# Stage tiles in two rings, and a smaller share for attention at a hand-over

## The chip, the cores and the metric

The kernel runs on one core of one Trainium2 chip, in one launch. The time is device microseconds from a run's start to its end, the median of several runs. The time of before is 606.85 us, the median of 3 runs (605.4 to 607.78).

## The reference

One input `x` (2048 tokens of 512 channels, fp32) goes through two branches that are mixed by a gate. Cut to what matters:

```python
g = sigmoid((x * gate_w).sum(-1, keepdims=True))
# branch A: 32 heads of 16; each token attends to 8 tokens, 2 apart
q, k, v = split(x @ wqkv)
idx = pos[:, None] - 2 * arange(8)[None, :]
logits = where(idx >= 0, (q * k[idx]).sum(-1) * 16 ** -0.5, -1e9)
a = ((softmax(logits)[..., None] * v[idx]).sum(window)) @ wo
# branch B: gated feed-forward (FFN), 512 -> 1792 -> 512
b = (gelu(x @ w_gate) * (x @ w_up)) @ w_down
out = g * a + (1 - g) * b
```

## The kernel before

**Halves.** The tokens are worked on in two halves, `par` 0 and 1 (the even and the odd of 16 tokens that share a partition), since a window with step 2 never leaves its half. The program runs `start()` (keys and queries of the first half), `ffn(0)`, `kq_second()` (keys and queries of the second half), `ffn(1)` and its end with the output projection.

**Matmuls.** Every fp32 operand is split into a high and a low part (`hi` on ScalarE, `lo` on VectorE), and a product is three matmuls: high by high, low by high, high by low. The gate and up products, the keys and queries, and the values are each computed with a seven-product scheme (Strassen and Winograd's), so that sums of weights and of products (`c12`, `c22` by `add`, L566; copies `p5` and `u2` by `copy`, L561) pass through ScalarE and VectorE between the matmuls.

**The FFN.** `ffn(par)` (L704) runs over 14 chunks of 128 hidden channels. `gate_up` (L620) issues the seven products of one chunk in four PSUM banks of ring `p`, with the Gelu (`c11`, L656; `ge`, L675) and `hidden` (L571: the product L572, its high part L574 on ScalarE, its low part L575 on VectorE) behind them. The seventh product is held back to the next chunk (`fourth`). From the third chunk on, four calls of `down` (L590; matmuls at L601) for chunks that are done lie between the products. After the last chunk eight more calls of `down` follow; their sums are scaled on ScalarE (L612 in the first FFN).

**Values.** In the first two chunks of each FFN the values of the same half are computed too, by `values` (L271) along `PLAN`. Each of four token tiles `t` has two stages of 512 columns. Each stage gets three of the scheme's seven steps and is stored to memory twice: `first` (L226) stores its left part, `second` (L231) its right one, to `vs`. `STAGES` (L197) says from which rings a tile's two stages are taken: tile 2 and tile 3 take both from ring `s`. The order of the steps is, chunk by chunk (letters are steps, figures are tiles; steps d, c and e use stage 0, steps b, f and g stage 1):

```python
PLAN = (("a0 b0", "c0 d0 a1", "e0 f0 d1", "b1 g0 c1", "e1 f1 a2", "d2 g1 c2 b2"),
        ("f2 e2 a3", "g2 d3", "b3", "c3 e3", "f3", "g3"))
```

**Rings.** A ring is a fixed number of tiles of one size: `s` has 4 (512 columns), `c` has 4 (544 columns). A new tile can be written when all that used an old one of its ring is done, stores to memory included. Ring `s` serves `p5` and `u2` of every chunk; ring `c` serves `c11`, `c12`, `c22` and `ge` of every chunk, and four raw weight tiles of the values.

**Attention.** It is one long generator, `attention` (L422), over eight units (half, quarter of the channels), nearly all on VectorE. A unit has `scores` (four steps: a product L324 and a reduction L327), a softmax, and `mix` (L371; four steps: a product L386, then sums L390, L392, L394; a transpose and a store after every second). Each step yields about its cost in us: 4.6 for a step of the scores, 2.3, 1.2 and 1.1 for a step of `mix`, 0.7 for a transpose. The generator also loads: `load_kq` brings a unit's keys and queries, ahead of time if they are there.

**Who gets how much.** Everywhere in the program, `pull(budget)` (L464) adds to a credit and draws the generator until the credit is used up; `pull(1e9, key)` draws until a unit is done, and sets the credit to 0. In the FFN the budget is a fixed number times `PACE`: 0.9 in the first chunks and 1.0 later in the first FFN, 1.12 in the second. The last chunk of the first FFN has a further 0.8 in `gate_up`. In `kq_second` the blocks ask as `ASK` says. The products L324 and L386 also wait for the last matmul that was traced before them (`paced`, `LAST`), so the place in the program is a hard bound for them.

**The order on each engine** is made ahead of the run by a scheduler with a simulated timeline. It takes what is ready by its place in the program, with attention's instructions 150 places later (`BEHIND`), and deals out the tiles of the rings; the engines then run their queues in that order.

**Around the hand-over.** `ffn(0)` ends with eight `down` calls. Four of them accumulate in ring `p`, which the next stage needs too: `kq_second` (L1252) computes a first block (24 matmuls into the `acc` banks), copies the sums into four banks of `p` on ScalarE (`out_of`, L937) and adds a second block there (24 matmuls, `a12` by `b21`). Keys of the first columns are then copied to tile `kq` by `put` (L1279). The same tile holds the values that units (0, 0) to (0, 2) mix from.

Of the kernel before, what the change touches and what calls it, by code (L numbers as in the profile page):

```python
# [22 lines left out]
FC = F // P  # L23
# [8 lines left out]
NU = D // UC  # L32
# [1 line left out]
FILLERS = 2  # L34
ASK = (0.3, 0.3, 0.3, 0.6, 1.0, 1.2, 1.2)
BEHIND = 150
PACE = (0.9, 1.0, 1.12)
LOAD = 4.0
BT = 4
MASKED = -1e9 * DH ** 0.5  # L40
# [8 lines left out]
def tile_gated_mix(ctx: ExitStack, tc: tile.TileContext, xt, wqkv, wff, wo, out):  # L49
# [11 lines left out]
    def tl(tag, dt=F32):  # L61
        return pool.tile([P, COLS.get(tag, 512)], dt, name=tag, bufs=BUFS[tag])
# [5 lines left out]
    def bank(tag):  # L68
        return psum.tile([P, 512], F32, name=tag, bufs=BUFS.get(tag, 1))
# [7 lines left out]
    for i in range(WARM):  # L77
        c = i // 4 % 2 * QW
# [115 lines left out]
            VR["t4"] = VR["b21"]  # L194
            sub(VR["t4"], VR["b21"], VR["t2"])

    STAGES = (("r", "r"), ("hh", "hl"), ("s", "s"), ("s", "s"))  # L197

    def value_steps(par, t):

# [14 lines left out]
        def staged(i):  # L215
            if ("s", i) not in T:
                T["s", i] = tl(STAGES[t][i])[:, :512]
            return T["s", i]
# [72 lines left out]
    def load_kq(par, u):  # L291
        hh, c = divmod(u, 2)
        k, q = slots_of(u > 0), KQ["a"][:, 2 * NP - 1:]
        if u == 1:
            q = pool.tile([P, 2, BT * UC], F32, name="tb").rearrange("p a (b c) -> p (a b) c", c=UC)
        LG[par, u] = k, q
        if not u:
            return
        loads = load_slots(k, KS[par, hh][c])
        loads.append(nc.sync.dma_start(q, QS[par, hh][c].rearrange("(p j) d -> p j d", j=NP)))  # L300
        if not par and 1 < u < NU - 1:
            for ins in loads:
                after(ins, SCORED[-1])
        elif (par, u) == (1, 2):
            after(loads[-1], PEAK[-1])
# [13 lines left out]
    def scores(par, u):  # L319
        k, q = LG[par, u]  # L320
        lg = pool.tile([P, UH, NP, W], F32, name="lg", bufs=2)
        for jj in range(0, NP, 2):
            prod = pool.tile([P, 2, W, UC], F32, name="prod")
            paced(nc.vector.tensor_tensor(prod, spans(k, jj), q[:, jj:jj + 2, None, :].to_broadcast([P, 2, W, UC]),  # L324
                                          op=OP.mult))
            yield 2.3
            nc.vector.tensor_reduce(two_of(lg, jj), prod.rearrange("p j w (h d) -> p (j w) h d", d=DH), axis=AX.X,  # L327
                                    op=OP.add)
            yield 2.3
        first = lg[:1, :, :NP - 1, :W - 1]  # L330
        SCORED[:] = [nc.vector.tensor_tensor(
            first, first, mask[:1, None, :NP - 1, :W - 1].to_broadcast([1, UH, NP - 1, W - 1]), op=OP.min)]
        LG[par, u] = lg
# [71 lines left out]
    done = set()  # L405
# [9 lines left out]
    def ordered(ins, other):  # L415
        after(ins, other, mybir.DependencyClass.NoSync)

    def need(*key):
        while key not in done:
            yield None  # L420

    def attention():  # L422
        units = [(0, u) for u in range(NU)] + [(1, u) for u in range(NU)]
        yield from need(0, 0)
        load_kq(0, 0)
        load_kq(0, 1)
        yield from scores(0, 0)
        yield from scores(0, 1)
        yield from need(0, 1)
        scored, mixed = 2, False  # L430
        for i, un in enumerate(units):
            if scored == i:
                yield from need(un[0], un[1] // 2 * 2)
                load_kq(*un)
                if un[1]:
                    yield LOAD
                else:
                    load_kq(un[0], 1)
                yield from scores(*un)
                scored += 1  # L440
                mixed = False
            yield from softmax(*un)
            if un == (1, 0):
                yield from scores(*units[scored])
                scored += 1
                yield from need(un[0], 1)
            yield from gated(*un)


            to = units[scored] if scored < len(units) else None  # L450
            ahead = to and (to[0], to[1] // 2 * 2) in done
            if ahead:
                load_kq(*to)
            yield from mix(*un, LOAD if mixed else 0.0)
            done.add((*un, "o"))
            mixed = not ahead
            if ahead:
                yield from scores(*to)
                scored += 1

    fill = attention()
    credit = [0.0]

    def pull(budget, key=None):  # L464
        credit[0] += budget
        while credit[0] > 0 and (key is None or key not in done):
            with tc.high_priority(offset=-BEHIND):
                c = next(fill, None)
            if c is None:
                credit[0] = 0.0  # L470
                return
            credit[0] -= c
        if key:
            credit[0] = 0.0
# [105 lines left out]
    def pace(par, f):  # L580
        return PACE[2 if par else f > 5]

# [4 lines left out]
    NG = FC // 2  # L587
    out_v = out.rearrange("(p j) d -> j p d", j=NT)

    def down(par, gr, t, b):  # L590
        if b == t == gr == 0:
            ACC.update((t, bank(f"acc{t}")) for t in range(BT))
        pp = bank("p") if b else ACC[t]
        if b and gr:
            nc.scalar.activation(pp, RT[BT + t], AF.Copy)
        ts = slice(t * P, (t + 1) * P)
        for i in range(2):
            hh_, hl_ = Hs[2 * gr + i, b]
            d = WD[2 * gr + i]
            for n, (a, w) in enumerate(((hh_, d[:, :512]), (hh_, d[:, 512:1024]), (hl_, d[:, :512]))):  # L600
                ins = nc.tensor.matmul(pp, a[:, ts], w, start=(i == 0 and n == 0 and gr == 0),  # L601
                                       stop=(i == 1 and n == 2), skip_group_check=True)
                if gr and b == t == 0 and not par:
                    ordered(ins, LAST[-1])
                LAST[:] = [ins]
        jj = BT * b + t
        if gr == NG - 1 and par:
            nc.scalar.activation(pp, pp, AF.Copy, scale=gc[:, par, jj:jj + 1])
            ACC[jj] = pp
        elif gr == NG - 1:  # L610
            st = tl("rt" if b else "scss"[t])[:, :512]
            nc.scalar.activation(st, pp, AF.Copy, scale=gc[:, par, jj:jj + 1])  # L612
            nc.gpsimd.dma_start(out_v[2 * jj], st)
        elif b:
            if gr == 0:
                RT[BT + t] = tl("rt")
            nc.scalar.activation(RT[BT + t], pp, AF.Copy)  # L617
        pull(1.2 * pace(par, 2 * gr + 2))

    def gate_up(par, f, pieces, do, extra):  # L620


        w = {op: WG.pop((f, op)) for ops in GROUPS for op in ops}

        def idle(i, n):
            for x in do.get(i, ()):
                x()
            pull(n * pace(par, f) * (1.0 if par or f + 1 < FC else 0.8))

        def piece(i):  # L630
            for x in pieces[i]:
                x()

        idle(0, 0.0)
        X_ = bank("p")
        product(X_, "a11", w["b11"], True)
        W_ = bank("p")
        nc.scalar.activation(W_, X_, AF.Copy)
        next(extra, None)
        idle(1, 0.7)  # L640
        piece(0)
        Z_ = bank("p")
        product(Z_, "s1", w["t1"], True)
        p5 = copy(Z_)
        idle(2, 0.3)
        fourth()
        next(extra, None)
        product(X_, "s2", w["t2"], False)
        u2 = copy(X_)
        next(extra, None)  # L650
        idle(3, 0.7)
        piece(1)
        idle(4, 0.5)
        product(W_, "a12", w["b21"], False)
        c11 = tl("c")[:, :512]
        nc.scalar.activation(c11, W_, AF.Gelu_apprx_tanh)  # L656
        next(extra, None)
        idle(5, 0.7)
        product(Z_, "s4", w["b22"], False)
        c12 = add(Z_, u2)  # L660
        next(extra, None)
        idle(6, 0.5)
        piece(2)
        product(X_, "s3", w["t3"], False)
        c22 = add(X_, p5)
        hidden((f, 0), c11, c12)
        next(extra, None)
        idle(7, 0.7)
        piece(3)
        idle(8, 0.0)  # L670

        def last():
            product(X_, "a22", w["t4"], False)
            ge = tl("c")[:, :512]
            nc.scalar.activation(ge, X_, AF.Gelu_apprx_tanh)  # L675
            hidden((f, 1), ge, c22)
        late.append(last)
# [134 lines left out]
    def need_o(par, u):  # L812
        pull(1e9, (par, u, "o"))
# [133 lines left out]
    def out_of(o, ps):  # L947
        act.activation(o, ps, AF.Copy)
# [303 lines left out]
    def kq_second():  # L1252
# [35 lines left out]
        block(U, "s2", "t2", False, ask=ASK[2])  # L1288
        for t in range(BT):
            out_of(u2[t], U[t])  # L1290
        for t in range(2):
            put(t, V_[t])
        both(hi, "t4")
# [113 lines left out]
```

## Time and profile before

| | |
|---|---|
| median of 3 runs | 606.85 us |
| profiled execution | 601.95 us |
| its span, first to last instruction | 600.2 us |
| granted TensorE clock | 1.000 |
| TensorE (PE) busy | 587.3 us, 98% |
| weight loads (PEld) busy | 488.1 us, 81% |
| VectorE (DVE) busy | 540.0 us, 90% |
| ScalarE (ACT) busy | 391.2 us, 65% |
| DMA | 134.18 MB, mean 224 GB/s |

The profile is of one execution. PE is TensorE with its matmuls, PEld its weight loads, DVE VectorE, ACT ScalarE, POOL GpSimd, SP SyncE; a q behind an engine means its queue of DMA issues. A row of a timeline has start, duration (both in us), engine, line, operation, output and inputs with their sizes, and in brackets the idle time of the engine ahead of it with what ended that. A row of the chain of work that ended last has start, duration and what ran. A row of a stretch has the stretch in us, its length, the busy time of each engine with its count of instructions, the granted clock, and the DMA engines' busy share and GB/s.

### The profile page before, as it was taken

Reading aid. Unit: us, or ns where it says so; the run is one execution under the profiler, and the core shown is the slowest. Engines: PE = TensorE matmul, PEld = TensorE weight load, DVE = VectorE, ACT = ScalarE, POOL = GpSimd, SP = SyncE. Lnnn points to the kernel's source line nnn. Section 1 sums busy time; section 2 is a strip of 40 time slices with the busy share of each in tenths; the row PEclk is TensorE's granted clock in tenths of the full one; section 3 lists DMA queues with packets and bytes.
Section 4 is the critical chain, followed back from the end, with each engine's and each line's share of the span. In section 5 each row is a group of like instructions: output and inputs, shape, how many; then the busy total and the mean of one; then the engine's idle time right before and its main releaser. Section 6 shows DMA issues by size and latency. Waiting matters only on the chain.

```text
span 600.2 us, 8102 instructions
## 1 busy us (share of the span) xinstructions
PE 587.3 (98%) x2730; PEld 488.1 (81%) x2730; DVE 540.0 (90%) x644; ACT 391.2 (65%) x678; POOL 89.2 (15%) x121
## 2 busy tenths in 40 slices
PE   8999999999999999999899999999999999999997
PEld 6888978878887888877788888788888888888886
DVE  5998989879999899989989999899999899799972
ACT  5857646787776967785874346768666766785532
POOL 0501002111211111201117000111111111101200
PEclk9999999999999999999999999999999999999999
DMA  8778969898999799896779886877798587737824
GB/s 315 245 233 235 297 195 254 226 287 225 258 254 283 199 274 239 225 331 243 229 220 274 241 211 183 225 210 181 192 236 261 146 219 219 225 95 203 128 66 158
DMA packets 79810, 134.18 MB, mean 224 GB/s; under 512 B 7964, under 2 KB 45210, under 8 KB 79512
## 3 DMA queue, kind: packets, MB, share of 16 engines
q1 hardware_dynamic: 64426, 98.72, 50.0%
q0 software_dynamic: 12576, 32.97, 28.2%
q10 hardware_dynamic: 2766, 1.96, 1.0%
q8 instruction: 21, 0.34, 0.2%
q14 instruction: 21, 0.17, 0.1%
HBM read 68.30 MB, written 38.86 MB: 179 GB/s over the span
## 4 chain that ended last, share of the span: by engine, by line
PE 86%; DMA 5%; issue 4%; ACT 2%; DVE 2%; POOL 0%; SPq 0%; DVEq 0%; POOLq 0%; ACTq 0%
PE p L558 40%; PE p L601 11%; PE acc L601 10%; PE acc L895 7%; PE p L895 5%; PE p L828 5%; PE acc L210 5%; PE acc L828 2%; DMA g<-raw 2%; DMA vs<-s 1%; DMA d<-r 1%; DMA raw<-xt 1%; ACT L675 0%; ACT L344 0%; DVE prod L386 0%
## 5 line engine op out<-in xcount | busy, mean ns | idle before, releaser
L558 PE MATMUL p<-S,g 128*128 128x512 f32 x672 | 168.9, 390 | 3.7 <-ACT s L563 2.7
L558 PEld LDWEIGHTS p<-S,g 128*128 128x128 f32 x672 | 125.0, 188 | 30.3 <-ACT s L563 3.4
L558 PE MATMUL p<-A,g 128*128 128x512 f32 x504 | 128.9, 390 | 1.1 <-DMA g<-raw 0.5
L558 PEld LDWEIGHTS p<-A,g 128*128 128x128 f32 x504 | 93.6, 188 | 21.3 <-DVE c L568 1.2
L327 DVE TENSOR_REDUCE lg<-prod 128x128 f32<-128x2048 f32 x32 | 73.0, 2281 | 0.1
L516 POOL DMA_DIRECT2D g<-raw x40 | 34.5, 862 | 227.7 <-ACT g L515 134.0
L601 PE MATMUL p<-d,hh 128*128 128x512 f32 x224 | 67.4, 389 | 0.0
L601 PE MATMUL acc<-d,hh 128*128 128x512 f32 x224 | 62.1, 390 | 0.7 <-DMA d<-r 0.7
L386 DVE TENSOR_TENSOR prod<-kq,lg 128x2048 f32<-128x2048 f32 x24 | 54.7, 2277 | 0.2
L601 PEld LDWEIGHTS acc<-d,hh 128*128 128x128 f32 x224 | 41.8, 188 | 9.7 <-DMA d<-r 1.1
L601 PEld LDWEIGHTS p<-d,hh 128*128 128x128 f32 x224 | 42.1, 188 | 8.8
L563 ACT ACTIVATE s<-p 128x512 f32<-128x512 f32 x56 | 32.9, 597 | 22.9 <-PE p L558 18.8
L520 ACT ACTIVATE g<-raw 128x1024 fp32r<-128x1024 f32 (+1 forms) x40 | 39.5, 987 | 12.1 <-PE p L558 9.4
L515 ACT ACTIVATE g<-raw 128x1024 fp32r<-128x1024 f32 (+1 forms) x40 | 39.3, 986 | 10.3 <-PE p L895 6.3
L545 POOL DMA_DIRECT2D d<-r x24 | 20.5, 855 | 147.0 <-ACT d L544 120.1
L601 PE MATMUL p<-d,hl 128*128 128x512 f32 x112 | 41.8, 389 | 0.0
L574 ACT ACTIVATE hh<-c 128x512 fp32r<-128x512 f32 x56 | 35.1, 628 | 9.9 <-DVE c L572 9.9
L575 DVE TENSOR_TENSOR hl<-c,hh 128x512 fp32r<-128x512 f32 x56 | 38.3, 683 | 3.7 <-ACT hh L574 3.6
L568 DVE TENSOR_TENSOR c<-p,s 128x512 f32<-128x512 f32 x56 | 38.1, 683 | 3.8 <-PE p L558 2.8
L572 DVE TENSOR_TENSOR c<-c 128x512 f32<-128x512 f32 x56 | 38.2, 682 | 2.2 <-ACT c L675 2.1
L617 ACT ACTIVATE rt<-p 128x512 f32<-128x512 f32 x48 | 27.7, 595 | 18.6 <-PE p L601 18.0
L390 DVE TENSOR_TENSOR prod<-prod 128x1024 f32<-128x1024 f32 x32 | 38.9, 1216 | 0.1
(203 smaller groups left out, 1016.0 us busy)
## 6 DMA issues: line engine op xcount, KB each, us to landing
g<-raw POOLq DMA_DIRECT2D x27, 512.0 KB, 6.1
raw<-wff SPq DMA_DIRECT2D x42, 256.0 KB, 4.0
ws<-g SPq DMA_DIRECT2D x14, 768.0 KB, 5.7
g<-ws SPq DMA_DIRECT2D x14, 768.0 KB, 5.3
r<-wff SPq DMA_DIRECT2D x28, 256.0 KB, 4.2
d<-r POOLq DMA_DIRECT2D x24, 256.0 KB, 6.2
g<-raw POOLq DMA_DIRECT2D x13, 384.0 KB, 6.3
os<-tb SPq DMA_DIRECT2D x64, 64.0 KB, 4.3
```

Source lines behind the costliest of these rows:

```text
L327: nc.vector.tensor_reduce(two_of(lg, jj), prod.rearrange("p j w (h d) -> p (j w) h d", d=DH), axis=AX.X, op=OP.add)
L386: paced(nc.vector.tensor_tensor(prod.rearrange("p j w (h d) -> p (j w) h d", d=DH), spans(v, jj).rearrange("p j w (h d) -> p j w h d", d=D ...
L390: nc.vector.tensor_tensor(prod[:, :, :4], prod[:, :, :4], prod[:, :, 4:], op=OP.add)
L515: nc.scalar.activation(lo, raw, AF.Copy, scale=-1.0)
L520: ins = nc.scalar.activation(hi, raw, AF.Copy)
L558: LAST[:] = [nc.tensor.matmul(ps, w_, a_, start=(start and kc == 0 and n == 0), stop=(kc == 1 and n == 2), skip_group_check=True)]
L568: nc.vector.tensor_tensor(c, ps, s, op=OP.add)
L572: nc.vector.tensor_tensor(ge, ge, up, op=OP.mult)
L575: nc.vector.tensor_tensor(hl_, ge, hh_.bitcast(F32), op=OP.subtract)
L601: ins = nc.tensor.matmul(pp, a[:, ts], w, start=(i == 0 and n == 0 and gr == 0), stop=(i == 1 and n == 2), skip_group_check=True)
L828: ins = nc.tensor.matmul(pa, a, b, start=(first and n == 0), stop=(last and n == 2), skip_group_check=True)
L895: return lambda *args, **kw: self.add(getattr(self.eng, name)(*args, **kw))
```

## The change

Stages: tile 2 takes its first stage from ring `s` and its second from ring `c`, tile 3 the other way round. Shares: in the last chunk of the first FFN the asks of `gate_up` are weighted 0.5 instead of 0.8, and those of the eight `down` calls after it 0.5 instead of 1. The second FFN's pace is 1.14 instead of 1.12. In `kq_second`, before the first new keys are copied to `kq`, attention is drawn until unit (0, 2) has been mixed. Unit (1, 0) is never loaded ahead.

```diff
-PACE = (0.9, 1.0, 1.12)
+PACE = (0.9, 1.0, 1.14)
+LAST_PACE = 0.5
...
-    STAGES = (("r", "r"), ("hh", "hl"), ("s", "s"), ("s", "s"))
+    STAGES = (("r", "r"), ("hh", "hl"), ("s", "c"), ("c", "s"))
...
-            ahead = to and (to[0], to[1] // 2 * 2) in done
+            ahead = to and to != (1, 0) and (to[0], to[1] // 2 * 2) in done
...
-        pull(1.2 * pace(par, 2 * gr + 2))
+        pull(1.2 * pace(par, 2 * gr + 2) * (1.0 if par or gr + 1 < NG else LAST_PACE))
...
-            pull(n * pace(par, f) * (1.0 if par or f + 1 < FC else 0.8))
+            pull(n * pace(par, f) * (1.0 if par or f + 1 < FC else LAST_PACE))
...
             out_of(u2[t], U[t])
+        need_o(0, NU - 2)
         for t in range(2):
             put(t, V_[t])
```

## The prediction

> **What bounds the kernel now.** I read the page's busy line first, then the waits of PE, then stretches by engine, and last the chain and the timelines at the places that these pointed to.
>
> ```profile
> PE 587.3 (98%) x2730; PEld 488.1 (81%) x2730; DVE 540.0 (90%) x644; ACT 391.2 (65%) x678; POOL 89.2 (15%) x121
> ```
>
> PE is busy for 587.3 of 600.2 us, so all that a change of order can win is 12.9 us of idle PE. The stretches show where (the columns are the stretch, its length, then busy time of PE, PEld, DVE, ACT, POOL):
>
> ```profile
> 0.00:20.00 20.00, 18.43 (x78) 13.93 (x79) 12.96 (x23) 13.02 (x27) 3.55 (x10) 1.00 0.89 323
> 580.00:600.00 20.00, 16.58 (x74) 13.40 (x72) 5.02 (x8) 3.41 (x6) 0.00 (x0) 1.00 0.37 132
> 285.00:582.00 297.00, 292.77 (x1365) 244.78 (x1366) 277.25 (x313) 189.50 (x330) 44.77 (x57) 1.00 0.74 200
> 520.00:582.00 62.00, 62.00 (x275) 51.34 (x275) 59.53 (x72) 38.05 (x67) 8.59 (x10) 1.00 0.58 126
> ```
>
> The start takes 20.00 - 18.43 = 1.57 us and the end 20.00 - 16.58 = 3.42 us; the change touches neither. About 7.9 us lies between. Three of those gaps are long, and a fourth will matter:
>
> ```profile
> 83.58 0.73 PE L558 MATMUL p<-S,g 128*128 128x512 f32 x2 [1.47 <-ACT s L563]
> 287.26 1.42 PE L895 MATMUL p<-g,A 128*128 128x512 f32 x5 [2.32 <-ACT p L895]
> 358.99 0.73 PE L558 MATMUL p<-S,g 128*128 128x512 f32 x2 [1.27 <-ACT s L563]
> 382.12 1.21 PE L601 MATMUL acc<-d,hh 128*128 128x512 f32 x4 [0.70 <-DMA d<-r]
> ```
>
> The first and third are the same gap, once in the second chunk of each FFN; the second is the hand-over from the first FFN to the second half's keys and queries. Together they hold 1.47 + 1.27 + 2.32 = 5.06 us, the ceiling of what the change can take away.
>
> **Part 1, the rings of the value stages.** In both FFNs the gap ends with the copy at L563, which puts a product into a tile of ring s. In the first FFN the chain and ACT's timeline say what the copy itself waited for:
>
> ```profile
> 76.39 6.43 DMA vs<-s
> 82.92 0.60 ACT L563 ACTIVATE s<-p 128x512 f32<-128x512 f32 x1 [2.53 <-DMA vs<-s]
> ```
>
> Ring s has four tiles. In program order the first chunk takes two (p5, u2) and two for the stages of tile 2; the second chunk then wants p5, u2 and two more for tile 3. A staged tile comes free only when both of its stores have landed, and ACT stood 2.53 us for such a store. After the change ring s is asked for p5, u2, one half of tile 2, p5, u2, one half of tile 3, p5, u2. The second u2 then finds the first chunk's p5 or u2, both long added up, or the fourth tile. So the copy waits for no store: 1.47 us go in the first FFN, and by the same count 1.27 us in the second.
>
> Ring c pays: four tiles, asked for by c11, c12, c22 and ge of every chunk, now with two staged halves more. Counting live tiles, the tight place is c11 of the third chunk: the earlier c11 is still read, c22, ge and a half of tile 3 hold the rest.
>
> ```profile
> 92.87 0.60 ACT L656 ACTIVATE c<-p 128x512 f32<-128x512 f32 x1 [0.54 <-PE p L558]
> 92.69 0.67 DVE L575 TENSOR_TENSOR hl<-c,hh 128x512 fp32r<-128x512 f32 x1
> vs<-s SPq DMA_DIRECT2D x12, 128.0 KB, 4.4
> ```
>
> L656 would wait until L575 ends, 92.69 + 0.67 - 92.87 = 0.49 us, with ACT's queue behind it; PE is not waiting there, and would lose at most that. At worst a c tile is held for a store (the last column, 4.4 us to landing in the median) and the loss eats the whole gain; at best it is nothing. I take 0.2 us in each FFN, near the row with its place. Removing the gap also brings the down weights' split on ACT and DVE close behind PE, so I leave nothing more for it. Part 1: 2.74 - 0.4, about 2.3 us.
>
> **Part 2, half the share in the last chunk.** The seven asks of a chunk (0.7, 0.3, 0.7, 0.5, 0.7, 0.5, 0.7) sum to 4.1. In the last chunk of the first FFN they were weighted 0.8 (3.28), now 0.5 (2.05); its four downs ask 1.2 each as before (4.8); the eight downs after it asked 9.6, now 4.8. The sum falls from 17.68 to 11.65, by 6.03 us of VectorE work. One step of the mixing costs 2.3 + 1.2 + 1.1, 4.6, and 0.7 more after every second. Unit (0, 2) starts to mix with this chunk, so its third step is due after 9.9 and its fourth after 14.5 of the sum. Before, 8.08 were asked ahead of the eight downs, so the third step comes with the second down (2.4 more) and the fourth with about the fifth. After, 6.85 are asked, so the third step needs 3.05 / 0.6, the fifth or sixth down, and the fourth passes the hand-over: 2.85 are missing and the next block asks 0.3 eight times, so it lands behind that block's end.
>
> Each step's first product (L386) waits for the last matmul traced ahead of it. What VectorE does now at the hand-over:
>
> ```profile
> 275.01 0.65 DVE L572 TENSOR_TENSOR c<-c 128x512 f32<-128x512 f32 x1
> 275.69 2.29 DVE L386 TENSOR_TENSOR prod<-kq,lg 128x2048 f32<-128x2048 f32 x1
> 277.90 0.68 DVE L895 TENSOR_TENSOR g<-S,g 128x512 fp32r<-128x512 f32 x1
> 278.50 1.22 DVE L390 TENSOR_TENSOR prod<-prod 128x1024 f32<-128x1024 f32 x1
> 280.84 0.68 DVE L575 TENSOR_TENSOR hl<-c,hh 128x512 fp32r<-128x512 f32 x1
> 278.75 0.64 ACT L574 ACTIVATE hh<-c 128x512 fp32r<-128x512 f32 x1
> ```
>
> Between the last hidden product (L572) and its low part (L575) stand 2.29 + 1.22 us of the third step. After the change that step waits for a down's last matmul, which itself needs this low part, so it cannot stand ahead of it. L575 is then bound by ScalarE's high part L574 at 278.75 + 0.64, some 1.4 us earlier, and by up to 3.5 us if L574 moves too. The chain shows what that is worth:
>
> ```profile
> 282.68 1.36 PE acc L895 x6
> 284.04 0.24 PE p L601
> 284.30 0.69 ACT rt L612 x2
> 285.46 1.27 ACT rt L612 x2
> 286.72 0.50 ACT p L895
> 287.26 5.77 PE p L895 x24
> ```
>
> The low parts' matmuls come last on PE, behind the whole first block of the next stage; then ScalarE drains four banks and copies the sums into the first of them, and PE stands still. With L575 earlier, the low parts go ahead of some of that block, and the block hides the drains. Six matmuls moved (1.36 us) cover 1.36 us of the 2.32; ten and more cover all. I take 1.7 us, between these. Bounds: 2.32, and below nothing minus one L386 (-2.29), should the late fourth step stand in front of a low part that PE needs.
>
> **Part 3, the rest.**
>
> ```profile
> 285.32 2.29 DVE L386 TENSOR_TENSOR prod<-kq,lg 128x2048 f32<-128x2048 f32 x1
> 299.01 0.38 ACT L895 ACTIVATE kq<-p 128x256 f32<-128x256 f32 x1
> ```
>
> The pull that finishes unit (0, 2) ahead of the new keys replaces what the pace had done; its VectorE work, a fourth step, moves from 285.32 to after the second block there, 287.26 + 5.77 = 293.03, and crosses no queue but SP's stores of its output. The first copy of new keys waits for that step's L386 and stands at 299.0, so 6 us hide its 2.29. The test on (1, 0) chooses what was chosen before, since those keys weren't there: nothing. The second FFN asks for 4.1 in each of 14 chunks and 1.2 in 56 downs, 124.6; 0.02 more gives 2.49 us. Adding up the shares step by step, attention is 1.4 us behind after the forced pull, 2.3 at the second FFN's start, and 1.1 ahead at its end, with the last unit's steps at the same matmuls as before. What that meets there:
>
> ```profile
> 588.42 0.69 DVE L88 TENSOR_TENSOR hl<-raw,hh 128x512 fp32r<-128x512 f32 x1 [6.50 <-ACT hh L87]
> 591.66 0.62 PE L828 MATMUL p<-S,hh 128*128 128x512 f32 x2
> ```
>
> The last low part of attention is done at 589.11 and PE first needs it at 591.66: 2.55 us of slack. Cost: none.
>
> The other small gaps (0.70 us at 382, and what is left of the 7.9) have causes that move with PE, so I leave them. Sum: 2.3 + 1.7 = 4.0 us. The profiled execution took 601.95 us around its span of 600.2; it would take about 598.0 with a span of 596.2. The median of the runs shown is 606.85, 4.9 above the profiled one; I carry the difference over: 606.85 - 4.0 = 602.85 us. A measurement of this kernel can tell about 0.5%, 3.03 us, from no change.
>
> **Rivals.**
>
> *Only the rings work.* The order at the hand-over is fixed ahead of the run, and the low parts could stay last. Then 2.3 us remain: 604.5. For it: ScalarE runs L574 3.1 us after its input was there (275.01 + 0.65), so VectorE was not all that held it. Against: the step that stood in the way cannot stand there any more.
>
> *VectorE is the bound and keeps its times.* Then PE can gain only until the last unit's low part is late: 2.55 us, so 604.3. For it: 59.53 of 62.00 us busy at the end. Against: PE is 62.00 of 62.00 busy in the same row, and VectorE's steps wait for matmuls, so they move along.
> In the Trainium skill, Perfetto Trace Analysis, section Identifying the Most-Contended Engine, TensorE is judged by weight loads rather than matmuls, and the engine with the highest occupancy is the one to work on. By that rule VectorE (90%) would stand ahead of TensorE (81%), and this rival would be the forecast; the trace so far speaks the other way, since the idle 12.9 us of matmuls are what is left.
>
> *The rings don't do it.* The tiles are handed out by a simulated schedule, and c may hold a tile where s did: then 2.74 us stay and 1.7 go: 605.15. Little speaks for it but the tight count of c.
>
> *Slower: attention ends late.* The place is the last unit; the mechanism, that the 6.03 us put off are not made good before it, so that VectorE's last low part sets the end. It decides from 2.55 us on, and costs 6.03 - 2.55 = 3.5 us, with PE's own gains lost: 610.35. Against it, VectorE has 297.00 - 277.25 = 19.75 us idle from 285 to 582, and the raised pace gives 2.49 of it; for it, those idle times are small ones between waits.
>
> **How the numbers follow.** Forecast 0.53, only the rings 0.18, VectorE's bound 0.12, rings without effect 0.06, slower 0.11. The forecast's own range is 601.3 to 604.4 (its bounds 5.06 and 2.3 us, with some spread of the other gaps). The range for all takes in the next three cases and reaches half a microsecond below the ceiling of 601.8, since other gaps may close too: 601.0 to 606.4; the slower case and the edges are left out. Faster by over 0.5% means under 603.82: most of the forecast (0.46) and an edge of the two cases at 604.4 (0.10), 0.56. Slower by over 0.5%, above 609.88: 0.07. The same: 0.37.
>
> **What would show it.** Right: no wait of L563 for vs<-s, no PE gap near 82 and 356; L575 ahead of any L386 at the hand-over, a PE gap under 1 us before the second block there, the last low part still ahead of PE. Wrong: a wait of L656 or L568 for a store of c, a gap at the hand-over as long as now, or PE waiting near the end for hl<-raw.

## The result and the profile after

The kernel after takes 597.4 us (597.08 to 598.43, 4 runs), the kernel before beside it 606.42 us (605.4 to 607.78, 4 runs): a ratio of 0.9853, 95% interval 0.9829 to 0.9877. The gain is 9.0 us where 4.0 were forecast. Timed twice more, the same two kernels were nearer together: 0.9898 (0.986 to 0.9936) and 0.9889 (0.9863 to 0.9915). The profiled executions, though, differ by almost what was forecast: 601.95 and 597.21 us, 4.7 apart. Why the medians differ by more than the profiles is the question of this case. Two runs of 1527 and 1201 us, one of the kernel after with the old pace and one with tile 3 alone changed, are left out below; why they took so long isn't known.

The page of the kernel after:

```profile
span 595.4 us, 8113 instructions
PE 586.5 (98%) x2730; PEld 488.2 (82%) x2730; DVE 538.5 (90%) x644; ACT 391.1 (66%) x678; POOL 89.3 (15%) x121
```

PE now stands idle for 595.4 - 586.5 = 8.9 us, 4.0 less than the 12.9 of before. (The other 0.8 us of span are busy time, 587.3 against 586.5.) The stretches of after say where the idle time went:

```profile
80.00:100.00 20.00, 19.76 (x97) 16.47 (x96) 19.80 (x25) 12.16 (x23) 2.54 (x3) 1.00 0.70 207
100.00:120.00 20.00, 17.90 (x79) 14.48 (x78) 16.46 (x18) 11.87 (x20) 3.43 (x4) 1.00 1.06 292
280.00:300.00 20.00, 20.00 (x90) 16.52 (x89) 20.00 (x30) 15.41 (x30) 3.22 (x6) 1.00 0.55 191
300.00:320.00 20.00, 18.93 (x94) 15.89 (x93) 17.98 (x25) 11.97 (x26) 7.53 (x10) 1.00 0.92 262
340.00:360.00 20.00, 20.00 (x132) 18.32 (x131) 19.37 (x22) 12.07 (x28) 0.92 (x1) 1.00 0.90 264
380.00:400.00 20.00, 20.00 (x90) 16.57 (x89) 18.99 (x20) 13.58 (x22) 2.54 (x3) 1.00 0.90 239
```

The first busy column is PE. The idle 1.47 us between 80 and 100 are down to 0.24, and the stretches with the gaps at 287, 359 and 382 are full: every gap that the prediction quoted has closed. But two are new, 2.10 us between 100 and 120 and 1.07 between 300 and 320, where the same two stretches of before read 20.00:

```profile
100.00:120.00 20.00, 20.00 (x90) 16.57 (x89) 18.47 (x21) 14.84 (x23) 4.26 (x5) 1.00 0.90 219
300.00:320.00 20.00, 20.00 (x91) 16.59 (x90) 17.47 (x23) 11.43 (x26) 6.62 (x9) 1.00 0.80 229
```

The waits of PE in the kernel after (line, what it waited for, then total us, times, longest) name the two new ones, and none for `s` (not shown is one of 1.1 us at the start, for `zero`):

```profile
PE acc L602 <- DMA d<-r: 2.1, 1, 2.1
PE acc L211 <- ACT acc L225: 1.1, 1, 1.1
PE p L559 <- DMA g<-raw: 0.6, 1, 0.6
```

(From line 37 on, line numbers are one higher after the change.) ScalarE's timeline of after shows the copies into ring `s` at the place of the first old gap, and `c11` of the third chunk:

```profile
85.63 0.60 ACT L564 ACTIVATE s<-p 128x512 f32<-128x512 f32 x1 [1.53 <-PE p L559]
88.81 0.60 ACT L564 ACTIVATE s<-p 128x512 f32<-128x512 f32 x1 [2.57 <-PE p L559]
96.49 0.61 ACT L657 ACTIVATE c<-p 128x512 f32<-128x512 f32 x1
```

L564 now waits for PE alone. The copy that had waited 2.53 us for `vs<-s` waits for its product instead, and `c11` waits for nothing that the profile shows.

### The profile page after: what moved, and what is told of

Read it like the earlier page. It is cut to its first block, busy times and chain, and to the rows that moved or that the text cites. A ratio compares the mean times of both kernels' runs of the same rounds, so it can differ in the third digit from the quotient of the medians.

```text
span 595.4 us, 8113 instructions
## 1 busy us (share of the span) xinstructions
PE 586.5 (98%) x2730; PEld 488.2 (82%) x2730; DVE 538.5 (90%) x644; ACT 391.1 (66%) x678; POOL 89.3 (15%) x121
## 4 chain that ended last, share of the span: by engine, by line
PE 86%; DMA 5%; DVE 4%; issue 3%; ACT 1%; POOL 1%; SPq 0%; POOLq 0%; ACTq 0%
PE p L559 43%; PE acc L602 12%; PE p L602 12%; PE acc L211 6%; PE p L829 5%; PE acc L896 4%; PE p L896 3%; PE acc L829 2%; DMA g<-raw 1%; DMA d<-r 1%; DVE S L896 1%; DMA raw<-xt 1%; DMA ks<-hh 1%; DVE prod L387 1%; DMA raw<-wff 1%
## 5 line engine op out<-in xcount | busy, mean ns | idle before, releaser
L602 PE MATMUL acc<-d,hh 128*128 128x512 f32 x224 | 60.3, 390 | 2.1 <-DMA d<-r 2.1
L564 ACT ACTIVATE s<-p 128x512 f32<-128x512 f32 x56 | 33.0, 600 | 16.6 <-PE p L559 16.3
L569 DVE TENSOR_TENSOR c<-p,s 128x512 f32<-128x512 f32 x56 | 37.6, 682 | 4.8 <-PE p L559 2.9
L576 DVE TENSOR_TENSOR hl<-c,hh 128x512 fp32r<-128x512 f32 x56 | 38.3, 684 | 3.6 <-ACT hh L575 3.3
L575 ACT ACTIVATE hh<-c 128x512 fp32r<-128x512 f32 x56 | 35.1, 630 | 7.5 <-DVE c L573 7.0
```

The costliest lines, as they stand in the source:

```text
L569: nc.vector.tensor_tensor(c, ps, s, op=OP.add)
L576: nc.vector.tensor_tensor(hl_, ge, hh_.bitcast(F32), op=OP.subtract)
```

## The experiments

Four groups were run, each on one chip and with runs of the kernel before among them. Those medians were 603.81 us (20 runs), 603.88 (14), 603.39 (25) and 603.63 (15), all lower than the 606.42 beside the first result.

### The kernel before, once more

No edit.

> The kernel before, once more, with a profile of its own. Its profiled execution took 601.95 us while its other runs took 605.4 to 607.78. Theory A: the ordinary execution loses some 4 us more at one of the waits that the change removes (a copy at L563 waiting for a store of a stage, or the hand-over), so a profile at 605 to 607 us shows one of those gaps longer, by 3 to 5 us. Rival B: the 4 us lie somewhere that the change does not touch by design (another DMA wait, a clock below 1), and the changed kernel escapes them through its other order. Ratio 1.00.

Measured: 602.54 us (600.3 to 605.32, 10 runs), ratio 0.9993 (0.9963 to 1.0023). Two runs of one kernel can differ by 5 us, more than the change was forecast to win. Its profile (602.85 us, clock 0.996) shows how that comes about, first in the waits of PE, then in a stretch:

```profile
PE acc L601 <- DMA d<-r: 2.5, 1, 2.5
PE p L895 <- ACT p L895: 2.3, 1, 2.3
PE p L558 <- ACT s L563: 1.3, 2, 1.1
```

```profile
380.00:400.00 20.00, 18.15 (x74) 14.97 (x75) 14.02 (x15) 12.84 (x20) 2.42 (x3) 0.91 0.62 177
```

The wait for `d<-r` near 382, 0.70 us in the first profile, is 2.5 here, and in that stretch the granted clock is 0.91 instead of 1.00. So it is rival B: another DMA wait, and a clock below 1. In the trace's record of the clock it goes to one half for 3.413 us, from 381.44, just before the gap ends at 381.85: up to 3.413 / 2 = 1.7 us are lost, on top of the gap. One such fall among 601 us makes a mean of 1 - 1.7 / 601 = 0.997. The clock is at one half a second time from 599.89 on, when PE's last matmul is over (597.49); that costs no matmul, but brings the mean of this run down to 0.996.

Each run comes with its mean clock. Read by this profile, 0.999 is less than one fall among the matmuls, 0.996 and 0.997 are one, and lower values more. Of 84 runs of the kernel before (the 74 in the four groups and these 10) 16 had a clock of 1.000 and took 601.20 us in the mean, 7 had 0.999 (602.9 us), 43 had 0.996 or 0.997 (603.9) and 18 less (605.5). The prediction was made from a profile of the rarer kind, without a fall.

### The rings alone

```diff
-    STAGES = (("r", "r"), ("hh", "hl"), ("s", "s"), ("s", "s"))
+    STAGES = (("r", "r"), ("hh", "hl"), ("s", "c"), ("c", "s"))
```

> Only the stages of tiles 2 and 3 in rings s and c; shares as before. Theory A with the rings as the place of the extra loss: 606.4 - 2.7 - 4 = about 599.5 us. If the extra loss sits at the hand-over instead: 606.4 - 2.4 = 604 us, and the gap of 2.3 us at 285 us is still there. Rival B: no telling, between 601 and 606.

Measured: 599.44 us (598.69 to 600.91, 10 runs), 0.9935 (0.9906 to 0.9964). The surprise is in PE's timeline at the hand-over:

```profile
275.99 1.98 PE L601 MATMUL p<-d,hh 128*128 128x512 f32 x8
277.81 1.07 PE L601 MATMUL p<-d,hl 128*128 128x512 f32 x4
278.71 5.60 PE L895 MATMUL acc<-g,A 128*128 128x512 f32 x24
```

All low parts of the downs (`hl`) are now ahead of the whole first block, whose 24 matmuls hide ScalarE's drains: the gap of 2.32 us is gone though no share was changed. VectorE shows the same order:

```profile
274.37 0.69 DVE L575 TENSOR_TENSOR hl<-c,hh 128x512 fp32r<-128x512 f32 x1 [0.70 <-ACT hh L574]
275.74 2.29 DVE L386 TENSOR_TENSOR prod<-kq,lg 128x2048 f32<-128x2048 f32 x1 [0.68 <-PE acc L601]
```

The third step of the mixing stands behind the low part here as well. The orders on the engines are made ahead of the run, on a simulated timeline; that a change of two rings 200 us earlier shifted it enough for another order is the likely reading, but that timeline isn't on record. At a clock of 1.000 these runs took 599.10 us in the mean (4 runs), 2.1 less than before. The largest changes add up to as much: 2.74 and 2.32 gone, a new wait for `d<-r` of 1.9 and one for L224 of 1.1. Smaller gaps changed too: in the two profiles PE's idle time is 12.9 and 597.2 - 587.3 = 9.9 us, 3.0 less. The median is the 599.5 that theory A gave, by luck: the other profile of the kernel before has no gap that is 3 to 5 us longer, and a part of the gain came at the hand-over.

### The shares alone

The kernel after with the old `STAGES` and the pace at 1.12:

```diff
-PACE = (0.9, 1.0, 1.14)
+PACE = (0.9, 1.0, 1.12)
...
-    STAGES = (("r", "r"), ("hh", "hl"), ("s", "c"), ("c", "s"))
+    STAGES = (("r", "r"), ("hh", "hl"), ("s", "s"), ("s", "s"))
```

> Only the smaller share in the last chunk with the forced pull and the test on (1, 0); stages in s as before, pace 1.12. By the prediction the hand-over's gap of 2.32 us goes and the two waits for ring s stay: 606.4 - 2 = 604.4 us. If the extra 4 us sit at the hand-over: about 600. Slower rival: with no raised pace the last unit ends later, up to 2.5 us are hidden; a PE wait for hl<-raw near the end would show it.

Measured: 609.79 us (607.39 to 611.95, 4 runs), 1.0128 (1.0086 to 1.0171): slower. PE's timeline at the hand-over:

```profile
276.26 4.24 PE L896 MATMUL acc<-g,A 128*128 128x512 f32 x18
280.34 1.98 PE L602 MATMUL p<-d,hh 128*128 128x512 f32 x8
282.15 1.52 PE L896 MATMUL acc<-g,A 128*128 128x512 f32 x6
283.51 1.07 PE L602 MATMUL p<-d,hl 128*128 128x512 f32 x4
286.90 1.68 PE L896 MATMUL p<-g,A 128*128 128x512 f32 x5 [2.32 <-ACT p L896]
```

and VectorE's:

```profile
279.23 0.68 DVE L576 TENSOR_TENSOR hl<-c,hh 128x512 fp32r<-128x512 f32 x1
283.94 2.29 DVE L387 TENSOR_TENSOR prod<-kq,lg 128x2048 f32<-128x2048 f32 x1 [0.76 <-PE p L602]
```

The forecast was 604.4 here. The low part did move ahead of the third step, to 279.23 from 280.84: 1.6 us earlier, where 1.4 was forecast. But PE still has its four `hl` matmuls behind the block, so being ready earlier wins nothing, and the gap stays at 2.32. A fall follows it: the stretch 280 to 300 has a clock of 0.91 in this run's trace. In the second FFN things are worse. PE, ScalarE and SP's queue there:

```profile
364.63 2.92 PE L559 MATMUL p<-S,g 128*128 128x512 f32 x6 [3.79 <-ACT s L564]
```

```profile
363.98 0.60 ACT L564 ACTIVATE s<-p 128x512 f32<-128x512 f32 x1 [5.49 <-issue]
```

```profile
352.22 2.81 SPq L402 DMA_DIRECT2D os<-tb  x3
358.90 0.34 SPq L301 DMA_DIRECT2D tb<-qs  x1
359.34 0.39 SPq L229 DMA_DIRECT2D vs<-s  x1
359.77 0.46 SPq L234 DMA_DIRECT2D vs<-s  x1
```

Attention that was put off issues its output stores (L402) and a load (L301) here, ahead of the stores of a staged tile (L229, L234). VectorE had written the half that L234 stores by 356.81, 3 us before its issue. From 359.77, the 4.4 us that such a store takes to land lead to 364.2, about where L564 ends its wait of 5.49 us. The profile names no releaser ("issue"), so this cause is put together from the times, not shown. PE's gap grows to 3.79 us, and behind it the clock is at one half for 6.8 us (0.83 in the stretch 360 to 380). With the fall at the hand-over, 10.2 us at half speed cost 5.1 us. With the rings in place the same shares, pull and test do no such harm. The three were not run apart.

### The kernel after with the old pace

```diff
-PACE = (0.9, 1.0, 1.14)
+PACE = (0.9, 1.0, 1.12)
```

> The changed kernel with 1.12 instead of 1.14. If the raised pace only keeps the last unit from being late, this is within 1.5 us of the changed kernel (597.4): up to 599. If the pace itself brings the gain beyond the prediction: 601 to 602.5 us.

> The changed kernel with the pace of 1.12 in the second FFN, beside the changed kernel. If the raised pace does nothing at the end, as the prediction has it (2.55 us of slack): within 1 us of it. The first look gave 596.35 here, 1 us less than the changed kernel on another chip. If the raised pace is worth its 2.49 us: 599.5 to 600.

Measured: 596.35 us (596.24 to 598.16, 5 runs), 0.9912 (0.9881 to 0.9943); again, beside the kernel after, 598.3 us (597.27 to 598.56, 4 runs), 0.9903 (0.9869 to 0.9937). The kernel after itself in that group:

> The changed kernel on the same chip as the three beside it, as their yardstick. Theory A2, after the first four runs: the undisturbed times (granted clock 1.000) differ by the gaps of the prediction, some 4 us (before 601.1), and the rest of the difference between the medians is the clock, which falls to a half for 3.4 us after a long gap of PE; so nearly all runs of this kernel have a clock of 0.999 or more, and its median is 597 to 598 us. Rival: chips differ, and this one shows 2 us or more of spread.

It took 597.09 us (596.66 to 598.12, 4 runs), 0.9898 (0.986 to 0.9936). So the old pace was 1.2 us slower beside it, where within 1 us was expected; three of its four runs have a clock of 0.996 or 0.997, against one of the four here. In the ratios to the kernel before the intervals overlap almost wholly, and the pace cannot be told from none. The other way round, the kernel before with 1.14 as its only edit:

> Only the second FFN's pace of 1.14; rings and shares as before, and the hand-over's order is that of the kernel before. The prediction gave this part nothing by itself: ratio 1.00, the gaps of the kernel before in the profile. Rival: the raised pace alone delays or frees something in the second FFN, over 2 us either way.

Measured: 603.64 us (601.34 to 605.93, 10 runs), 0.9995 (0.997 to 1.0019), with the gaps of before.

### One tile alone

```diff
-    STAGES = (("r", "r"), ("hh", "hl"), ("s", "s"), ("s", "s"))
+    STAGES = (("r", "r"), ("hh", "hl"), ("s", "s"), ("c", "s"))
```

> Only tile 3 takes its first stage from ring c; all else as before. Counted by live tiles, u2 of the second chunk then finds a tile of s, so the waits of L563 for stores go (2.7 us); but the program's fixed order at the hand-over is that of the kernel before (18 of the next block's matmuls ahead of the last downs' low parts), so its gap of 2.3 us stays, and with it the clock's falls there. Theory A2: undisturbed runs 598 to 599 us, median about 600, some runs with a clock under 0.998. Rival, the hand-over does not matter: like the rings on both tiles, 599.4, clock as there.

Measured: 602.39 us, the median of 9 runs (599.74 to 604.31), 0.9969 (0.9943 to 0.9994). Its waits of PE:

```profile
PE p L895 <- ACT p L895: 2.3, 1, 2.3
PE p L558 <- DMA g<-raw: 2.1, 1, 2.1
PE acc L210 <- ACT s L224: 1.4, 1, 1.4
```

This is 2.4 us more than the 600 that were expected. The wait at L563 is gone here too, but 1.4 us come back at L224, the evacuation of the values into a staged tile of `s`, which itself stood 2.60 us for a store `vs<-s` in ScalarE's timeline: the wait has moved from one user of the ring to another. The hand-over keeps its old order and its 2.3 us, as expected, and a wait for `g<-raw` of 2.1 us at 195 is new; the one fall in this profile comes behind that, at 196. So tile 3 alone is not enough, for the stage or for the hand-over. Tile 2 alone was not tried.

### The new gap taken away

The wait for `d<-r` at 104 us is for the first down weights of the third chunk. GpSimd issued that DMA at 98.86, and it needs 7.43 us (kernel after, GpSimd's timeline, the chain, and PE's timeline):

```profile
98.86 0.85 POOL L546 DMA_DIRECT2D d<-r  x1 [1.10 <-ACT d L545]
```

```profile
98.86 7.43 DMA d<-r
```

```profile
106.34 0.98 PE L602 MATMUL acc<-d,hh 128*128 128x512 f32 x3 [2.10 <-DMA d<-r]
```

98.86 + 7.43 = 106.29, and PE goes on at 106.34. The edit starts these weights two places earlier in the chunk:

```diff
-                    at(4 if f == 2 else 0 if f % 2 and not par else 2, next, steps, None)
+                    at(2 if f == 2 else 0 if f % 2 and not par else 2, next, steps, None)
```

> The changed kernel with the third chunk's down weights (line 734 of the changed kernel) begun at place 2 instead of 4. The changed kernel has a new PE gap of 2.1 us at 104 us, which waits for their accumulating DMA (7.4 us, issued at 98.9). If that wait is what is next late behind the rings: the gap shrinks by what the issue moves, 1 to 2 us, and the time is 595.5 to 596.5. Rival: the issue is bound by tiles of ring d or by ScalarE's queue, and nothing moves: 597.4.

> The earlier down weights on the changed kernel again, beside the changed kernel, to tell 0.7 us from nothing (596.36 against 597.09, four runs each). If the gap of 2 us at 104 us costs its length and now and then a fall: 0.7 to 1.5 us faster than the kernel beside it and fewer runs below 0.999. Rival: the gain is given back at 130 us, less than 0.5 us.

> The changed kernel, as the yardstick for the three beside it: 597.1 us, about three in eight of its runs with a fall of the clock, by its gap of 2.1 us at 104 us.

Measured: 596.36 us (595.73 to 597.15, 4 runs), 0.9881 (0.9849 to 0.9913), against 597.09 for the kernel after in the same group. Again, in the fourth group: 596.22 (595.49 to 597.06, 6 runs), 0.9875 (0.985 to 0.99), against 597.06 (596.18 to 598.24, 6 runs), 0.9889 (0.9863 to 0.9915). This is the fastest version, by 0.7 to 0.8 us in both groups, though the intervals overlap. The second time the DMA was issued 11.3 us earlier than in the profile above (GpSimd's timeline), and the wait is gone from PE's list, whose top is now:

```profile
87.57 0.85 POOL L546 DMA_DIRECT2D d<-r  x1 [14.55 <-ACT d L545]
```

```profile
PE p L80 <- DVE zero L74: 1.1, 1, 1.1
PE acc L211 <- ACT acc L225: 1.1, 1, 1.1
PE acc L896 <- ACT g L896: 0.4, 1, 0.4
```

The wait closed is 1.9 us in the fourth group's run of the kernel after, the gain 0.8; PE's idle time there went from 595.1 - 586.8 = 8.3 us to 594.4 - 586.7 = 7.7. So most of it came back. In the stretches of the two profiles 0.6 us of it lie between 120 and 140, the place that the rival named (waits for L569 and L575 at 131 and 133), and 0.7 in the first 20 us, far from the edit. Nine of the ten runs of the two groups had a clock of 1.000.

### A gap put back

If gaps cause the falls, a gap of known length in the kernel after must bring them back. Extra copies of a finished sum at the hand-over into the first bank, on ScalarE, hold up the second block. With 4, 7 and 10 extra copies (the range is 5, 8 and 11) on the kernel after:

```diff
-        for t in range(BT):
-            out_of(V_[t], U[t])
+        for t in range(BT):
+            for _ in range(5 if t == 0 else 1):
+                out_of(V_[t], U[t])
```

> The changed kernel with a PE gap put back at the hand-over: the first of the four copies of the first block's sums (L938) is made five times over instead of once, so the second block waits some 4 x 0.56 us less the 1.4 us that the copies are ahead now: a gap of about 0.9 us. Theory A2 (a gap costs its length, and beyond some 2 us also falls of the clock to a half for 3.4 us): 597.1 + 0.9 = 598, clock 0.999 or more in nearly all runs. Rival (a gap costs only its length): the same here.

> The same with seven more copies: a gap of about 2.5 us, that of the kernel before. Theory A2: a part of the runs has a clock of 0.997 or less and is 1.7 us slower than the rest; undisturbed 599.6, median 600 to 601. Rival: 599.6 and clock 1.000 throughout.

> The same with ten more copies: a gap of about 4.2 us. Theory A2: every run has the clock's fall, for 3.4 or 6.8 us at a half, so 597.1 + 4.2 + 1.7 to 3.4 = 603 to 604.7. Rival: 601.3 and clock 1.000.

The gaps that they made, one kernel each:

```profile
284.46 1.42 PE L896 MATMUL p<-g,A 128*128 128x512 f32 x5 [1.01 <-ACT p L896]
```

```profile
285.89 1.66 PE L896 MATMUL p<-g,A 128*128 128x512 f32 x5 [2.85 <-ACT p L896]
```

```profile
287.70 2.50 PE L896 MATMUL p<-g,A 128*128 128x512 f32 x5 [4.68 <-ACT p L896]
```

Measured: 598.79 us (598.13 to 599.75, 4 runs; 0.9906, 0.9874 to 0.9938), 602.42 (601.29 to 605.41, 10 runs; 0.9987, 0.9961 to 1.0013) and 605.55 (603.87 to 606.75, 10 runs; 1.0016, 0.9998 to 1.0035). At 1.0 us two of four runs stayed at 1.000, and two had 0.997, which theory A2 did not expect; at 2.85 and 4.68 none of ten stayed at 1.000, and the last took 0.9 us more than the upper end of what was expected. But the gap of some 2.0 us at 104 is in these kernels too, so the kernel without it is the cleaner base. The same with 4 and 6 extra copies there:

> The kernel with the earlier down weights (no gap over 1.1 us after the start) with four more copies at the hand-over: a gap of 1.0 us and nothing longer. If falls of the clock need a gap near 2 us or more: all runs at 0.999 or more, about 597.4 us. If gaps of 1 us do it too (2 of 4 runs had one with gaps of 1.0 and 2.0): a third or more of the runs at 0.997.

> The same with six more copies: one gap of about 2.2 us. If such a gap brings a fall in a part of the runs: runs of two kinds, 598.5 at 1.000 and 600.2 at 0.997, in shares that the runs show; with 2.85 us it was ten of ten. If 2.2 us never does it: 598.5 throughout.

Measured: 598.11 us (596.66 to 598.65, 6 runs; 0.9903, 0.9877 to 0.9929) and 600.65 (598.93 to 601.79, 10 runs; 0.994, 0.992 to 0.996). With a gap of 1.0 us the clock was 1.000 in five runs and 0.999 in one. With 2.24 us it was 0.997 in eight runs of ten (600.73 us in the mean) and 1.000 in two (599.06 in the mean): 1.7 us apart, as one fall should cost. The gaps themselves cost a little more than their length: at 1.000 the base without them took 596.23 us, with 1.0 us put in 598.01 and with 2.24 us 599.06. One of the eight in PE's timeline:

```profile
285.07 2.29 PE L896 MATMUL p<-g,A 128*128 128x512 f32 x5 [2.24 <-ACT p L896]
...
290.90 1.29 PE L896 MATMUL p<-g,A 128*128 128x512 f32 x5
```

Five matmuls like these take 2.29 us right behind the gap and 1.29 three groups later.

## Why the prediction was right in its sum and wrong in its time

**The sum.** Compared at a clock of 1.000, the kernel before takes 601.20 us (16 runs) and the kernel after 597.03 (9 of its 14 runs that list a clock). The difference is 4.2 us, against a sum of 4.0. (With the runs at 0.999, which lost no whole fall either, it is 601.7 against 597.0, 4.7 us.) The forecast of 598.0 for the profiled execution met 597.21. The sum owes its fit partly to luck, as the parts below show.

**The step that failed: "4.9 above the profiled one; I carry the difference over".** It took the distance from the profiled execution to the median for an offset that an edit leaves alone. It isn't one. (The profiled 601.95 lies below all three runs whose median it was set beside, 605.4 to 607.78.) On the experiments' chips the distance from the runs at 1.000 was 603.6 - 601.2 = 2.4 us, and most of it is falls of the clock, which follow PE's gaps: the 84 runs have a clock of 0.9968 in the mean, which is 1.9 us of 601. The rest goes with gaps that are longer in some runs, as the one at 382. The gaps gone, most falls go: in the kernel after 3 of 14 runs had one, and the median is 597.16, 0.1 above its runs at 1.000. So a gap of 2.3 us costs its length, some tenths more, and about 1.7 in each run in which a fall came behind it. Of the 9.0 us of the first result, 4.2 are the difference without falls, and some 2.3 (2.4 less 0.1) what falls and longer gaps add in the other groups. The last 2.5 are the distance from 603.6 to 606.42 for the kernel before, on that chip, less 0.3 for the kernel after; the clock of those runs of before isn't listed, so whether they were more falls stays open.

**Part 1, the rings: right.** Both waits of L563 for stores vanished. The 0.4 us set aside for ring `c` was not asked for: no copy into `c` waits for a store, nor `c11` for L576. The count of live tiles found the tight place but not its slack. What was missed is a price elsewhere: in the order made for the new rings PE comes to the third chunk's down weights before they have landed, for 1.9 to 2.1 us of waiting. (The kernel before issued a load of `d` at 100.82 and shows no wait of PE between 100 and 120.)

**Part 2, the share: its first half right, its conclusion wrong.** The third step left the place ahead of the low part and that came 1.6 us earlier (forecast 1.4). The step "with L575 earlier, the low parts go ahead of some of that block" failed: with the shares alone PE's order was the old one, and the gap 2.32. The gap did close, wholly where 1.7 was taken, but through the rings. The kernel with the rings alone and the one with the shares alone could tell this apart; the kernel after alone would have seemed to bear the step out. Why two rings change the order 200 us later is open, and forcing the hand-over's order alone was not tried. That its gap was what cost the time there is shown from the other side: put back, it cost the time again.

**Part 3: right as far as it was tested.** The pace cannot be told from none, and with the rings in place pull and test brought no wait near the end. They were not run alone.

**The small gaps.** "I leave them" was a mis-sized term: those at 132, 256 and 382 (0.52, 0.95 and 0.70 us, by the busy time of their stretches) closed, two others of 2.10 and 1.07 opened. By the stretches of the two profiles 7.0 us of idle time closed and 3.2 opened; that the balance is so near 4.0 is luck. With the rings in place, the shares with pull and test are worth about 2 us at a clock of 1.000 (599.10 against 597.03, and on one chip, with the old pace and the runs at 0.999 taken in, 599.11 against 597.04); 1.0 of it is idle time of PE in the profiles (9.9 against 8.9), and no run shows which of the three brings it.

**The rivals.** "Only the rings work" had the share right (no gain at the hand-over by itself) and the result wrong, since the rings close it. "VectorE is the bound" fell: its limit was 2.55 us, and 4.0 of idle PE are gone while VectorE's busy time is 538.5 (540.0 before). "The rings don't do it" did not happen; with tile 3 alone, though, 1.4 of the 2.74 us came back as a wait for the same ring at L224. "Slower: attention ends late" did not happen. The tail of after, VectorE and then PE:

```profile
584.00 0.69 DVE L89 TENSOR_TENSOR hl<-raw,hh 128x512 fp32r<-128x512 f32 x1 [6.47 <-ACT hh L88]
```

```profile
586.93 0.62 PE L829 MATMUL p<-S,hh 128*128 128x512 f32 x2
```

The last low part is done at 584.69, 2.24 us ahead of its matmul. The shares alone are slower, but by another road than this rival's: by gaps in the second FFN, put down above to SP's queue, and not at the end.

## What to carry to other kernels

Compare two kernels at equal granted clock first, then count how often each loses its clock; a single profiled execution may be one without the falls that the median has, and the distance between the two is not a constant. An idle gap of TensorE of about 2 us or more cost itself here and, often, half of 3.4 us more, so take the longest gaps first, and look for the ones that an edit opens elsewhere. Where the order is made by a planner, an edit in one place can reorder another: run each part alone before a gain is put down to it.

## What the runs showed of the hardware

The granted clock fell to one half for 3.413 us at a time, 1.7 us lost, and did so behind gaps shorter than that. By length of the longest gap in a kernel's profile: 1.0 us, no clock of 0.997 in 6 runs; 2.24, eight of 10 runs; 2.85, all 10; 4.68, all 10, with 6.83 us at half in the profiled one. (The last two kernels have the gap of 1.9 to 2.0 us at 104 besides.) Gaps of one length can go either way: 2.32 us in the first profile of before had no fall behind it, 2.32 in the kernel with the shares alone had one.

The traces show why. In every record of the clock the time between two changes is a whole multiple of 3.413 us (375.466 us is 110 of them, 279.893 is 82), so the clock changes on a grid whose place differs from run to run: the records begin 3.77 to 7.01 us after the first instruction. Here are two pairs of neighbouring steps of that grid in the second profile of the kernel before, the first with most of the gap of 2.32 us, the second with most of the one of 2.49:

```profile
282.46:285.88 3.42, 1.50 (x7) 0.92 (x5) 3.42 (x4) 2.57 (x5) 1.51 (x3) 1.00 0.18 35
285.88:289.29 3.41, 3.02 (x13) 2.50 (x14) 2.74 (x4) 3.41 (x8) 1.49 (x3) 1.00 0.90 285
378.03:381.44 3.41, 1.33 (x6) 0.75 (x4) 2.02 (x3) 3.37 (x5) 0.85 (x1) 1.00 1.06 340
381.44:384.86 3.42, 3.01 (x7) 2.44 (x8) 3.30 (x4) 2.08 (x5) 0.00 (x0) 0.50 1.04 267
```

With 1.9 us idle in one step the clock stays at 1.00, with 2.08 the next step has 0.50. The 17 traces with such a record agree. The end of the kernel left out, seven steps at full clock have 2.08 to 2.44 us of idle PE, and a fall follows each of them; all other steps at full clock have 1.93 us or less, and no fall follows one of them. So a gap of a little over 2 us brings a fall if it lies in one step, and none if the grid cuts it in two: the 2.32 us of the first profile were cut into 1.51 and 0.81, those of the shares alone lay in one step. This was read from the traces afterwards; no run was made to test it.

The Trainium skill, page TensorE: Matmul & The Clock Gate, section HAM oscillation — how this bites in real kernels, gives the rule that PE should have no idle gap over about 3.4 us; by it no gap of the kernel before would have cost its clock. The length of a fall agrees with that figure; the length of the gap that is needed does not, and here the measurement decides.
